# Attention with normalised queries and keys, then an MLP: a planned schedule gets another DMA model, new tables, and denser filler matmuls

## Chip, cores and metric

The kernel runs on one core of a Trainium2 chip. The metric is the device time of one execution in microseconds (us). A core has five engines that run side by side and wait for each other through semaphores: PE (TensorE, matrix products), DVE (VectorE), ACT (ScalarE), POOL (GpSimd) and SP (SyncE, which here only issues transfers). PEld is the loading of weights into PE, which overlaps its products.

## The reference

```python
def _attn_ref(q, k, v, g_q, g_k):            # 8 x 12 x 448 x 64
    q_n, k_n = rmsnorm(q, g_q), rmsnorm(k, g_k)
    scores = np.matmul(q_n, k_n.transpose(0, 1, 3, 2)) / np.sqrt(64)
    attn = softmax(scores)
    return np.matmul(attn, v)

def reference(...):
    x = attn_out.transpose(0, 2, 1, 3).reshape(3584, 768)
    h = x @ w_in                              # 768 x 2048
    g = h * np.clip(h + 3.0, 0.0, 6.0) / 6.0
    return g @ w_out                          # 2048 x 768
```

`rmsnorm` divides each row of 64 by the root of its mean square (plus 1e-06) and multiplies by the gains. All inputs and the output are float32.

## The kernel before

There are eight batches of twelve heads. Two heads make a pair, so there are 6 pairs in a batch and 48 in all. For a pair, q and k are loaded (`loads`), squared and summed over 64 elements (`prep`, L576 and L593), turned into reciprocal roots on ACT (L599, L600), scaled to bf16 (`qks`, L609 and L616), transposed into `kq` (on PE at L669 for the first two batches, by a DMA at L688 for the rest), and the keys with the gains become `kp`. The values are copied to bf16 with a column of ones (`va`). Scores S are products of `kp` with `kq` (L817), exponentials `e` are taken by ACT (L850), and `e` times `va` gives X with the sums of the softmax in the extra column (L906). DVE normalises X (`xn`, L924 and L925), and `xn` is transposed into `xT` (on PE at L946 for the first two batches, else by a DMA).

A sequence has 448 rows, 3 x 128 + 64. The last 64 keys of each pair, the rest, are handled apart: `kr` and `vr` are loaded for six pairs at once, `kb` holds the scaled rest keys, L822 makes their scores, `er` their exponentials and L788 their part of X.

The MLP of a batch runs on PE between the attention steps of the next one. An h group (L985) is 6 products of 384 or 512 columns into one of two M banks, followed by ACT (`t`, L991) and DVE (`gT`, L993). A y group (L1010) is 16 products of 384 columns, followed by a copy `y` and a store. The weights `w_in_sb` and `w_out_sb` are loaded by eight transfers of 768 KB of bf16 results that POOL issues (L500, L506); they convert from float32. All other transfers are issued by SP, except for two tiny ones for the gains by ACT.

The order is not written by hand. The kernel first records all work as steps (`add`), each with the engines that it may run on and what each costs, a due time and its dependencies. A planner, `Plan`, then simulates list scheduling: it goes forward in time, starts on each engine the ready step with the earliest due time, and repeats this with due times taken backward from the end. At the end three hand-fitted tables act on single steps by their number: `NUDGES` shifts a due time, `ENGINES` fixes the engine, `HOLD` sets the earliest start. The instructions are emitted in the planned order. On the chip each engine works through its list in this order and waits where a semaphore is not there yet. So the planner's times are not obeyed on the chip; only its order is.

The planner's picture of transfers is the class `Queues`. A transfer enters the engines `ENTER` = 1.15 us after its issue on SP, or `SOFT` = 2.0 us after on POOL. Transfers at the heads of different rings share the engines. When a POOL transfer comes up after a time without one, it has the engines for itself for `ALONE` packets per engine (18 the first time, 3 later).

Where the planned order leaves PE open for more than 0.2 us before 115 us, `fill` puts in zero matmuls (L1128): products of zeros into a part of a PSUM bank that nobody reads then, with 240 columns (in X) or 64 (in S). They keep PE busy. They have no data to wait for but stand in PE's list like all others, so they take their time whether the gap is there or not. `FILL` = 0.9 scales how many there are for a gap, `FILL_FROM` = 1.2 is where filling starts, and up to `COLD` = 7.0 us each counts double. Ahead of everything DVE sets `zero` (L1136) and three whole PSUM tiles, X, S0 and S1 (L1138), to zero.

Of the kernel before, what the change touches and what calls it, by code (L numbers as in the profile page):

```python
# [19 lines left out]


NUDGES = {
    9: -1709, 10: -818, 11: -16, 12: -13, 13: -178, 14: -247, 15: -51, 16: -1.32, 17: -134, 18: -210,
    20: -10.58, 21: -79, 22: -61, 33: -65.1, 34: -65, 36: 99, 38: 94, 41: 151, 42: 323, 47: -56, 52: 1, 53: -50,
    54: -11, 58: -56, 60: -444, 64: -31, 71: -15, 72: -12, 82: -3.5, 85: -1677, 98: 91, 110: 30, 138: 396,
    140: 946, 172: -194, 179: 112, 193: 197, 196: 33, 197: -208, 205: -525, 227: 20, 230: -1329, 241: -553,
    242: -347, 251: -1753, 277: -127, 283: 31, 288: 134, 289: 242, 291: 544, 295: 406, 301: -130, 338: 28,
    342: -80, 347: -703, 357: -294, 368: 9, 369: 377.5, 370: 375, 376: 243, 377: 229, 381: -2085, 383: -240,
    409: 72, 423: 734, 431: -357, 441: -5, 447: 108, 450: -678, 451: 112, 457: -140, 458: -110, 484: -5,
    489: -22, 491: -74, 498: -325, 499: -319, 501: -8, 521: -15, 522: -8, 528: 322, 536: 10, 537: 34, 552: -12,  # L30
    565: 19, 583: 2.3, 594: 27, 617: -9, 655: -22, 671: -643, 672: -92, 673: -81, 685: 4, 693: 22, 703: 32,
    705: -129, 706: -560, 718: 23, 720: 138, 740: 21, 769: -490, 770: -26, 771: -7, 773: 19, 783: -25,
    784: -760, 792: 22, 801: 57, 802: 25, 804: -54, 805: -11, 811: 13, 840: 43, 861: 23, 870: -194, 871: -56,
    885: -3, 906: -171, 916: 49, 963: -24, 965: -43, 982: 109, 1013: 36, 1029: 45, 1030: -62, 1041: -24,
    1042: -5, 1053: 3.5, 1108: -45, 1132: 15, 1135: -4, 1136: -16, 1146: -91, 1147: -129, 1177: -9, 1179: -4,
    1184: -97, 1204: 4, 1214: 3, 1232: -18, 1233: -8, 1251: -4, 1307: 6, 1337: 2.4, 1379: -16, 1384: -12,
    1387: -2, 1398: -5, 1401: -11, 1408: 11, 1410: 8, 1455: 26, 1468: -21, 1469: -14, 1470: -45, 1471: -10,
    1485: 5.3, 1495: -15, 1520: 6, 1530: -32, 1531: -18, 1562: -21, 1568: -10, 1585: 5, 1604: -15, 1633: -6,
    1649: 5, 1650: 12, 1664: 4, 1669: -47, 1676: 10, 1695: 5, 1697: 3, 1714: -12, 1715: -6, 1716: -4, 1721: -3,
    1722: -4, 1742: -6, 1756: -5, 1774: -1, 1844: -4, 1848: 11, 1855: -13, 1875: -6, 1876: -8, 1893: -6,  # L40
    1919: 8, 1924: -4, 1940: -2, 1984: -9, 1997: 10, 2003: 2, 2016: -11, 2026: -2, 2027: -2,
}
ENGINES = {
    55: "POOL", 56: "ACT", 57: "POOL", 61: "POOL", 69: "DVE", 70: "DVE", 75: "ACT", 76: "DVE", 79: "POOL",
    89: "ACT", 90: "ACT", 91: "DVE", 97: "DVE", 98: "POOL", 102: "POOL", 115: "DVE", 120: "POOL", 123: "DVE",
    124: "POOL", 128: "POOL", 138: "ACT", 152: "POOL", 156: "POOL", 176: "ACT", 177: "POOL", 180: "POOL",
    184: "ACT", 185: "DVE", 189: "ACT", 211: "ACT", 223: "DVE", 240: "DVE", 244: "ACT", 252: "DVE", 253: "DVE",
    272: "DVE", 273: "POOL", 293: "DVE", 314: "ACT", 335: "ACT", 345: "DVE", 346: "DVE", 366: "ACT", 369: "DVE",
    370: "DVE", 376: "ACT", 404: "ACT", 430: "DVE", 495: "ACT", 525: "ACT", 583: "POOL", 689: "POOL",
    774: "DVE", 833: "DVE", 948: "DVE", 1123: "DVE", 1188: "POOL", 1209: "DVE", 1218: "POOL", 1386: "POOL",  # L50
    1750: "POOL",
}
HOLD = {
    39: 42.73, 40: 33, 41: 32, 47: 1, 58: 1, 62: 19, 109: 38, 110: 44, 150: 27, 177: 33, 207: 37, 227: 62,
    270: 36, 271: 36, 282: 42, 320: 46.7, 326: 85.2, 327: 53, 337: 24, 360: 56, 366: 51.1, 394: 62, 409: 44,
    410: 64, 411: 68, 412: 87, 413: 81, 448: 14, 465: 62, 476: 69, 526: 16, 527: 21, 532: 32, 533: 87, 549: 83,
    550: 82, 555: 53, 556: 86.7, 604: 70, 610: 77, 611: 94, 624: 76, 635: 95, 636: 99, 653: 93.6, 658: 104,
    659: 105, 660: 132, 661: 136, 664: 100, 695: 84, 696: 101, 713: 37, 714: 99, 715: 109.7, 790: 110, 791: 85,
    796: 119, 797: 129.9, 798: 125.233, 817: 111, 818: 97, 827: 112, 872: 97, 882: 140, 883: 89, 884: 125,
    885: 130, 907: 134, 908: 121, 928: 141, 929: 148, 930: 118, 931: 118, 932: 137, 976: 125, 977: 148, 982: 54,  # L60
    984: 154.57, 985: 19, 1006: 146, 1007: 96, 1064: 173, 1069: 179, 1070: 164, 1071: 177, 1100: 180, 1141: 185,
    1155: 163, 1157: 158, 1175: 193, 1193: 141, 1194: 199, 1195: 164, 1196: 206, 1236: 200.38, 1246: 177,
    1248: 178, 1249: 204.4, 1266: 212, 1267: 216, 1286: 183, 1289: 236, 1322: 208, 1329: 229, 1349: 225,
    1370: 232, 1416: 235, 1439: 218, 1440: 213, 1453: 254, 1460: 240, 1461: 195, 1462: 237, 1463: 225,
    1464: 215, 1508: 230, 1516: 243, 1558: 245, 1561: 198, 1596: 266.3, 1601: 280, 1602: 273, 1603: 277,
    1604: 266.5, 1622: 272.97, 1673: 275, 1707: 273, 1726: 303, 1727: 316, 1768: 306, 1781: 303, 1799: 329.7,
    1854: 296, 1860: 288, 1861: 310, 1936: 333, 1937: 333,
}


class Step:
# [5 lines left out]
    def __init__(self, on, due, fn, deps, xfer, after, lock, late, n):  # L77
        self.on, self.due, self.fn, self.xfer, self.after, self.lock = on, due, fn, xfer, after, lock
        self.deps = list({id(d): d for d in deps if d is not None}.values())
        self.late, self.n = late, n  # L80
        self.eng = self.start = self.end = None


class Queues:

    ENTER, SOFT, DONE, FIRST, ROOM = 1.15, 2.0, 0.3, 2.9, 108
    EXTRA, BEHIND = 0.05, 0.6
    ALONE = 18, 3  # L90

    def __init__(self):
        self.now = self.FIRST
        self.rings = {"SP": [], "ACT": [], "POOL": []}
        self.issued = []
        self.alone, self.awake, self.wakes = 0.0, False, 0

    def issue(self, s, at):
        n, size = s.xfer[0:2]
        cost = size * 4.5e-5 if s.eng == "POOL" else 0.012 + size * 4.2e-5  # L100
        n += self.EXTRA / cost
        if len(s.xfer) > 2 and self.rings[s.eng]:
            n += self.BEHIND / cost
        self.rings[s.eng].append([s, n, cost, at + (self.SOFT if s.eng == "POOL" else self.ENTER)])
        if s.eng != "POOL":
            self.issued.append(s)

    def lane(self):


        if sum(s.xfer[-1] if len(s.xfer) > 2 else s.xfer[0] for s in self.issued if s.end is None) > self.ROOM:
            return None
        return self.issued[-8].end if len(self.issued) >= 8 else 0.0

    def advance(self, until):

        while True:
# [5 lines left out]
            if soft and not self.awake:  # L123
                self.alone = self.ALONE[min(self.wakes, 1)]
                self.wakes += 1
# [195 lines left out]
def kernel(  # L321
# [35 lines left out]
    def tiles(name, n, shape, dt=BF16, pool=const):  # L357
# [38 lines left out]
    S_r = Ring(tiles("S", 2, [128, 2, 512], FP32, psum))  # L396
    X_r = Ring(tiles("X", 1, [128, 2, 512], FP32, psum))
    M_r = Ring(tiles("M", 2, [128, 512], FP32, psum))
    idle = [(X_r, 0, X_r.bufs[0][:, 1, 272:512]), (S_r, 0, S_r.bufs[0][:, 0, S:512]),
            (S_r, 1, S_r.bufs[1][:, 0, S:512])]  # L400
# [1 line left out]
    plan = Plan(NUDGES, ENGINES, HOLD)  # L402
    add = plan.add

    FILL, FILL_FROM, FILL_TO, COLD = 0.9, 1.2, 115.0, 7.0
    XPE, TQ, MOVE = 2, 0.26, 12
    GATE, W_IN_AT, W_OUT_AT, W_STEP = 4, 6.0, 40.0, 4.3
    START, FIRST, PAIR = 9.0, 3.7, 2.1
# [725 lines left out]

    with tc.manual_schedule():
        nc.vector.memset(zero[:], 0.0)  # L1136
        for t in (X_r.bufs[0][:], S_r.bufs[0][:], S_r.bufs[1][:]):
            nc.vector.memset(t, 0.0)  # L1138
        holder, free = None, FILL_FROM
        for s in order:  # L1140
            if s.eng == "PE":
                if s.start < FILL_TO and s.start - free > 0.2:
                    fill(free, s.start - 0.1, s.start)
                free = s.end
            ins = s.fn(s.eng)
            if ins is not None and s.lock and s.eng in ("DVE", "POOL"):
                if s.eng == "POOL" and holder is not None:
                    tc.add_manual_dep(ins.ins, holder.ins.name, mybir.DependencyInfo(
                        mybir.DependencyClass.Sync, mybir.DependencyReason.DATA), reason="port")
                holder = ins if s.eng == "DVE" else None  # L1150
# [30 lines left out]
```

## Time and profile before

| | us |
|---|---|
| median of 9 executions | 436.12 (434.15 to 438.27) |
| the profiled execution | 434.81 |
| its span, first to last instruction | 432.9 |
| PE busy | 419.4 |
| first zero matmul on PE starts | 2.16 |
| first scores on PE start | 11.89 |
| first h group's products start | 44.1 |
| first y group's products start | 78.3 |
| last of the weight transfers issued | 53.5 |

The page of a profile gives the busy time of each engine and groups of instructions. Busy is the union of the instructions' durations, and a matmul's duration includes its way through the array (a zero matmul of 240 columns lasts 0.266 us, but 22 of them in a row take 2.43). A row in the timeline has start, length, engine, line, operation and count; in square brackets stands how long the engine was idle before it and what ended that. The start of the timeline reads:

```profile
0.83 0.16 DVE L1136 MEMSET zero<- 128x120 uint32 x1 [0.83 <-PEq L1165]
1.20 0.91 DVE L1138 MEMSET X<- 128x1024 f32 x1 [0.21 <-issue]
2.16 3.56 PE L1128 MATMUL X<-zero 128*128 128x240 bf16 x17 [2.16 <-DVE X L1138]
2.27 0.91 DVE L1138 MEMSET S<- 128x1024 f32 x1 [0.16 <-issue]
3.35 0.91 DVE L1138 MEMSET S<- 128x1024 f32 x1 [0.16 <-issue]
3.40 0.58 ACT L574 ACTIVATE sq<-kf 128x448 f32<-128x448 f32 x1 [1.38 <-DMA kf<-in_k_dram]
5.09 0.28 DVE L483 SCALAR_TENSOR_TENSOR grow<-grow 1x128 f32<-1x128 f32 x1 [0.78 <-DMA grow<-in_g_k_dram]
```

### The profile page before, as it was taken

To read this page: it belongs to the slowest core of one execution; us is meant where nothing else is said; L and a number is where in the kernel's file an instruction comes from. 1 tells how busy PE (TensorE), PEld (TensorE's weight loads), DVE (VectorE), ACT (ScalarE), POOL (GpSimd) and SP (SyncE) were. 2 spreads that over 40 slices of the span, in tenths; PEclk is the share of its full clock that TensorE was granted. 3 is DMA by queue.
4 is the path that set the end of the run, shared out by engine and by line. 5 is a ranking of instruction groups with operands and counts; after the bars stand their busy time and mean duration, and the time that the engine had idled before them with its cause. 6 is when DMAs were issued, how large, how long until landed. Compare 5 with 4: busy or idle time off the path is not lost.

```text
span 432.9 us, 10404 instructions
## 1 busy us (share of the span) xinstructions
PE 419.4 (97%) x4174; PEld 248.7 (57%) x4191; DVE 239.3 (55%) x465; ACT 249.7 (58%) x458; POOL 217.5 (50%) x273
## 2 busy tenths in 40 slices
PE   7988999999999999999999999999999999999995
PEld 5666666565456565655556566554556665644563
DVE  7786887346765574556664665356645454244300
ACT  5887877467883687427763767337765565023211
POOL 4657556786869453676755754744847400000000
PEclk9999999999999999999999999999999999999999
DMA  8999999869876959695697784776562712310122
GB/s 237 212 228 258 247 230 212 166 170 223 191 162 159 204 120 186 114 245 117 117 198 200 136 162 134 150 197 177 95 156 74 120 26 50 82 47 0 38 73 74
DMA packets 114840, 64.79 MB, mean 150 GB/s; under 512 B 71272, under 2 KB 111336, under 8 KB 114792
## 3 DMA queue, kind: packets, MB, share of 16 engines
q1 hardware_dynamic: 107488, 57.83, 59.2%
q0 software_dynamic: 7296, 6.29, 9.1%
q8 instruction: 33, 0.54, 0.5%
q14 instruction: 15, 0.12, 0.1%
q10 hardware_dynamic: 8, 0.00, 0.0%
HBM read 45.61 MB, written 11.01 MB: 131 GB/s over the span
## 4 chain that ended last, share of the span: by engine, by line
PE 85%; DMA 6%; DVE 4%; ACT 2%; issue 1%; POOL 1%; SPq 1%; POOLq 0%; DVEq 0%; ACTq 0%
PE M L985 28%; PE M L1010 28%; PE X L906 8%; PE S L817 7%; PE S L1010 4%; PE S L985 2%; DMA kr<-in_k_dram 2%; DMA qf<-in_q_dram 2%; PE S L822 2%; PE X L1010 2%; DMA vf<-in_v_dram 2%; PE X L985 1%; PE X L788 1%; DVE ssq L593 1%; ACT e L850 1%
## 5 line engine op out<-in xcount | busy, mean ns | idle before, releaser
L985 PE MATMUL M<-xT,w_in_sb 128*128 128x384 bf16 (+1 forms) x681 | 143.5, 349 | 1.5 <-DVE gT L993 0.7
L850 ACT ACTIVATE e<-S 128x896 bf16<-128x896 f32 x144 | 124.9, 914 | 21.7 <-PE S L817 21.4
L1010 PE MATMUL M<-w_out_sb,gT 128*128 128x384 bf16 x736 | 130.0, 326 | 0.0
L1010 PEld LDWEIGHTS <-gT 128*128 128x128 bf16 x896 | 84.9, 98 | 55.2 <-issue 0.7
L985 PEld LDWEIGHTS <-w_in_sb 128*128 128x128 bf16 x768 | 70.9, 98 | 62.9 <-issue 3.2
L993 DVE SCALAR_TENSOR_TENSOR gT<-t,M 128x384 bf16<-128x384 f32 (+1 forms) x116 | 71.0, 613 | 62.6 <-ACT t L991 61.5
L991 ACT ACTIVATE t<-M 128x384 f32<-128x384 f32 (+1 forms) x116 | 62.7, 540 | 64.8 <-PE M L985 63.9
L593 DVE TENSOR_REDUCE ssq<-sq 128x14 f32<-128x896 f32 (+1 forms) x49 | 51.6, 1061 | 5.9 <-POOL sq L576 4.9
L906 PEld LDWEIGHTS <-e 128*128 128x128 bf16 x1152 | 45.3, 98 | 14.0 <-issue 5.5
L576 POOL TENSOR_TENSOR sq<-qf 112x512 f32<-112x512 f32 (+1 forms) x43 | 43.8, 1023 | 15.9 <-DMA qf<-in_q_dram 9.7
L906 PE MATMUL X<-va,e 128*128 128x65 bf16 x1152 | 51.7, 194 | 0.1
L540 DVE COPY y<-M 128x384 f32<-128x384 f32 x38 | 21.2, 558 | 43.4 <-PE M L1010 43.4
L817 PE MATMUL S<-kq,kp 64*128 64x448 bf16 x288 | 41.2, 354 | 1.7 <-ACT e L850 1.1
L576 POOL TENSOR_TENSOR sq<-kf 128x384 f32<-128x384 f32 (+1 forms) x39 | 32.4, 835 | 18.7 <-DMA kf<-in_k_dram 6.8
L616 POOL TENSOR_TENSOR qks<-kf,rs 128x384 bf16<-128x384 f32 x36 | 29.9, 831 | 21.6 <-ACT rs L600 17.0
L625 POOL TENSOR_TENSOR qks<-qf,rs 112x512 bf16<-112x512 f32 x36 | 37.6, 1046 | 4.2 <-ACT rs L600 3.7
L540 POOL CAST va<-vf 128x384 bf16<-128x384 f32 x44 | 22.2, 508 | 30.9 <-PE X L906 13.9
L850 ACT ACTIVATE er<-S 128x896 bf16<-128x896 f32 (+1 forms) x27 | 22.5, 833 | 18.9 <-PE S L822 18.8
L691 POOL TENSOR_SCALAR kp<-kq,gp 128x384 bf16<-128x384 bf16 x16 | 20.7, 1295 | 14.2 <-PE S L817 10.2
L925 DVE TENSOR_TENSOR xn<-X,rd 128x384 bf16<-128x384 f32 x48 | 26.8, 558 | 1.9 <-DVE rd L924 0.2
L599 ACT ACTIVATE rs<-ssq 128x14 f32<-128x14 f32 (+1 forms) x49 | 10.5, 214 | 24.0 <-DVE ssq L593 23.7
L817 PEld LDWEIGHTS <-kp 64*128 64x128 bf16 x288 | 9.4, 94 | 21.2 <-issue 18.0
(80 smaller groups left out, 313.0 us busy)
## 6 DMA issues: line engine op xcount, KB each, us to landing
qf<-in_q_dram SPq DMA_DIRECT2D x48, 224.0 KB, 3.7
kf<-in_k_dram SPq DMA_DIRECT2D x36, 192.0 KB, 3.5
vf<-in_v_dram SPq DMA_DIRECT2D x36, 192.0 KB, 3.6
out_dram<-y SPq DMA_DIRECT2D x18, 192.0 KB, 3.1
w_in_sb<-in_moe_w_in_dram POOLq DMA_DIRECT2D x4, 768.0 KB, 12.9
w_out_sb<-in_moe_w_out_dram POOLq DMA_DIRECT2D x4, 768.0 KB, 19.0
kf<-in_k_dram SPq DMA_DIRECT2D x12, 224.0 KB, 5.2
vf<-in_v_dram SPq DMA_DIRECT2D x24, 96.0 KB, 8.9
```

Source lines behind the costliest of these rows:

```text
L540: return (nc.vector if e == "DVE" else nc.gpsimd).tensor_copy(out=out, in_=x)
L576: return engines[e].tensor_tensor(out=o, in0=x, in1=x, op=MULT)
L593: lambda i0=i0, i1=i1, rows=rows: nc.vector.tensor_reduce(out=ssq[0:rows, i0:i1], in_=sq[0:rows, i0:i1], axis=AX_X, op=ADD),
L616: return engines[e].tensor_tensor(out=qks[:, 0:NS].rearrange("p t (h d) -> p h t d", h=2), in0=kf[:, 0:KH].rearrange("p (h t) d -> p h t d ...
L625: return engines[e].tensor_tensor(out=qks[0:PT, NS:QB].rearrange("p t (h d) -> p h t d", h=2), in0=qf[0:PT].rearrange("p (h t) d -> p h t ...
L817: fns.append(lambda ps=ps, a=a, t=t, kp=kp, rhs=rhs: nc.tensor.matmul(out=ps[:, a, 0:S], lhsT=kp[a * 64:a * 64 + 64, t * 128:(t + 1) * 128 ...
L850: lambda dst=dst, ps=ps, w=2 if whole else 1: nc.scalar.activation(out=dst, in_=ps[:, 0:w, 0:S], func=EXP), s, *(AVW[P] if t < NS else AVR ...
L906: nc.tensor.matmul(out=X[:, a, s * E1:(s + 1) * E1], lhsT=e[:, t, a, c0:c0 + 128], rhs=va[:, a * NS + t, :], start=False, stop=(t == NS - ...
L985: nc.tensor.matmul(out=m[:, 0:n], lhsT=w_in_sb[:, kt, f * 128:(f + 1) * 128], rhs=X[:, kt, :], start=(kt == 0), stop=(kt == NKT - 1))
L991: r = add("ACT", 0.17 + n / 1200, due + span, lambda: nc.scalar.activation(out=t[:, 0:n], in_=m[:, 0:n], func=RELU, bias=0.5, scale=1.0 / ...
L993: g = add("DVE", 0.155 + n / 960, due + span, lambda: nc.vector.scalar_tensor_tensor(out=G[:, f, :], in0=t[:, 0:n], scalar=1.0, in1=m[:, 0 ...
L1010: nc.tensor.matmul(out=m[:, 0:HALF], lhsT=G[:, f, i * 128:(i + 1) * 128], rhs=w_out_sb[:, f, cols], start=(f == 0), stop=(f == NFT - 1))
```

## The change

Four things change. In the planner's model the first POOL transfer enters after 1.75 us and each later one after 3.7 us (`SOFT` was 2.0 for all), and `ALONE` is 21 and 4 packets instead of 18 and 3. The three tables are made anew under this model, so the order on all engines, and the engine of some steps, differs; no step is added or removed. `FILL` is 1.0 and `FILL_FROM` 0.8. And before the start only those parts of X, S0 and S1 are set to zero that the zero matmuls write: 240, 64 and 64 columns instead of three times 1,024. The three tables are cut here; nearly every entry of them changes.

```diff
@@ NUDGES, ENGINES, HOLD
-    9: -1709, 10: -818, 11: -16, 12: -13, 13: -178, 14: -247, 15: -51, 16: -1.32, 17: -134, 18: -210,
+    9: -4221, 10: -2412, 11: -102, 12: -96, 13: -179.2, 14: -317, 17: -179.6, 18: -272, 20: -107, 21: -106,
...
@@ class Queues
-    ENTER, SOFT, DONE, FIRST, ROOM = 1.15, 2.0, 0.3, 2.9, 108
+    ENTER, SOFT, DONE, FIRST, ROOM = 1.15, (1.75, 3.7), 0.3, 2.9, 108
     EXTRA, BEHIND = 0.05, 0.6
-    ALONE = 18, 3
+    ALONE = 21, 4
...
-        self.alone, self.awake, self.wakes = 0.0, False, 0
+        self.alone, self.awake, self.wakes, self.soft = 0.0, False, 0, 0
...
-        self.rings[s.eng].append([s, n, cost, at + (self.SOFT if s.eng == "POOL" else self.ENTER)])
-        if s.eng != "POOL":
+        enter = self.ENTER
+        if s.eng == "POOL":
+            enter = self.SOFT[min(self.soft, 1)]
+            self.soft += 1
+        else:
             self.issued.append(s)
+        self.rings[s.eng].append([s, n, cost, at + enter])
@@ the kernel
-    FILL, FILL_FROM, FILL_TO, COLD = 0.9, 1.2, 115.0, 7.0
+    FILL, FILL_FROM, FILL_TO, COLD = 1.0, 0.8, 115.0, 7.0
...
         nc.vector.memset(zero[:], 0.0)
-        for t in (X_r.bufs[0][:], S_r.bufs[0][:], S_r.bufs[1][:]):
+        for _, _, t in idle:
             nc.vector.memset(t, 0.0)
```

In the built kernels the zero matmuls stand as follows: before 108 of 240 columns and 174 of 64, after 134 and 86. The other 3,909 matmuls are the same ones in another order.

## The prediction

> **What bounds the kernel now.** I read the page's first two parts, then the stretches, then the chain and the waits of TensorE (PE).
>
> ```profile
> PE 419.4 (97%) x4174; PEld 248.7 (57%) x4191; DVE 239.3 (55%) x465; ACT 249.7 (58%) x458; POOL 217.5 (50%) x273
> ...
> PEclk9999999999999999999999999999999999999999
> DMA  8999999869876959695697784776562712310122
> ```
>
> PE is busy 97% of the span at full clock, no other engine above 58%. The next view cuts that by stretch (columns: stretch, length, busy us and instructions of PE, PEld, DVE, ACT, POOL, then clock, DMA share, GB/s):
>
> ```profile
> 0.00:11.89 11.89, 9.47 (x83) 7.16 (x84) 8.78 (x17) 6.14 (x15) 5.46 (x23) 1.00 0.86 235
> 11.89:78.00 66.11, 60.80 (x1058) 42.35 (x1058) 51.67 (x110) 53.49 (x108) 42.28 (x52) 1.00 1.19 229
> 78.00:120.00 42.00, 41.68 (x399) 23.27 (x401) 21.56 (x40) 28.68 (x53) 31.94 (x39) 1.00 0.84 186
> 120.00:400.00 280.00, 279.16 (x2477) 159.79 (x2487) 153.31 (x295) 154.68 (x271) 137.77 (x161) 1.00 0.60 132
> ```
>
> The same stretches, zero matmuls alone:
>
> ```profile
> 0.00:11.89 11.89, 8.74 (x54) 6.28 (x54) 1.00 0.86 235
> 11.89:78.00 66.11, 14.97 (x229) 10.93 (x228) 1.00 1.19 229
> 78.00:120.00 42.00, 0.04 (x1) 0.00 (x0) 1.00 0.84 186
> ```
>
> From 78 us on PE has no filler and, to 400, 1.2 us of idle: nothing is left to win there. Before 78 us it waits: until the first scores (11.89) nearly everything is filler; from there to 78 us 15.0 us are zeros and 5.3 us idle. In that stretch the DMA share is over 1. The chain says what it waits for:
>
> ```profile
> 17.52 7.55 DMA vf<-in_v_dram
> ...
> 64.22 9.09 DMA kr<-in_k_dram
> 73.45 0.83 POOL sqr L738
> ...
> 77.19 0.74 PE S L1128 x20
> ```
>
> and the list of waits shows how little of the 5.3 us is a named wait:
>
> ```profile
> PE X L1128 <- DVE X L1138: 2.2, 1, 2.2
> PE S L817 <- ACT e L850: 1.1, 3, 0.5
> PE M L985 <- DVE gT L993: 0.7, 2, 0.5
> ```
>
> So the end is: start of PE, plus fixed real work, plus what the order leaves open before 78 us. Each microsecond closed there moves the end.
>
> **What the Trainium skill says.** "TensorE: Matmul & The Clock Gate", section Back-to-back issue gap, gives N/2.4 + 2.5 ns warm and N/1.2 cold. The trace agrees: 22 zero matmuls of 240 columns took 2.43 us, less 0.27 for the last one's length, so 0.103 us each; 20 of 64 columns took 0.74, so 0.029; the first 17, cold, about 0.2. Part 1 of that page says that the clock rises after some 3.4 us of activity in a free-running window; here PE starts at 2.16, the twelve zeros from 5.84 still take 0.19 each and those from 8.45 0.103. "VectorE: DVE Perf Modes", section on zero memsets, says one cycle per element; the trace has 0.91 us for 1,024. "DMA: Bandwidth & Descriptors", section Queues, rings and completion order, says that the engines alternate between queues by packets. The trace differs where a weight transfer begins: from 18.8 to 20.6 us the software queue took 107.4% of the engines, the hardware queue 6.3%. This stretch is what ALONE and the entry delay SOFT describe.
>
> **The change part by part.** The instruction order of the built kernels gives counts, the trace durations.
>
> Memsets: X shrinks from 1,024 to 240 columns, S0 and S1 to 64 each. By the 0.91 us row, an estimate of 0.25 for X. It begins at 1.20, so PE starts at about 1.5 and not 2.16, and DVE is free at about 2.0, not 4.26. That alone brings nothing: what follows waits for the first loads (ACT's square at 3.40) and for the gains (DVE at 5.09).
>
> First scores: 54 zeros before (17, 12, 3, 22), 58 after (21, 11, 13, 13). PE: 1.5 + 21 x 0.2 = 5.7, the gain row, 11 zeros of which some 7 cold to 7.9; the first transposes, whose input POOL scales from 6.4 for 0.94, are ready by then; 13 x 0.103 to 9.6, second transposes, 13 x 0.103 to 11.3. DVE: two sums to 6.5, gp, a square to 7.3, kb after the transposes to 8.75, two sums of 1.08 to 10.9, the copy of kp (0.42) to 11.35. First scores near 11.5: -0.4 us, bounds -0.8 and +0.3 (kp is now last on a full DVE).
>
> Zeros after the first scores: before 54 of 240 columns and 174 of 64, 54 x 0.103 + 174 x 0.029 = 10.6 us; after 76 and 86, 10.3 us. Their sum hardly moves; their meaning does. FILL was 0.9, so 10.6 us of zeros stood for gaps of 24,096 columns / 2400 / 0.9 = 11.2 us; at 1.0, 23,744 columns stand for 9.9 us. So the open time of the order falls by 1.3 us. Each gap also keeps 0.1 us plus a remainder (I take 0.15): 26 gaps against 24, -0.3 us. As a check, 11.2 - 10.6 + 26 x 0.15 = 4.5 us, near the 5.3 us of idle: the run followed its order with only about 1 us lost beyond.
>
> Where: up to 116,000 real columns, which PE reached at 78 us, the zeros fall from 10.6 to 8.8 us, above all where the chain waited for kr: from 99,000 to 116,000 real columns 5,712 zero columns become 3,104. Both halves of kr are issued two to three places earlier on SP, and one of the two vf half-loads behind the 17.52 row too. But 15 zeros of 240 columns (9 and 6) come where before had none, in what were 100 to 115 us: 1.55 us given back, since zeros issue whether or not the data came.
>
> Filling gaps whole: 64-column zeros cost 0.029 against the planned 0.0267, 86 x 0.0023 = 0.2 us too long, hidden by the 0.1 us margin of each gap; without it, +0.2.
>
> Entry delay and ALONE: no instruction of their own. Later weights are believed to enter at 3.7 us instead of 2.0, so data is planned later around them. Worth nothing if the old belief was right, and up to the 1 us of unplanned idle above if wrong. I take -0.2.
>
> Work moved between engines (both keys and queries of the first pair now POOL; kp, kb, xT copies traded between ACT and DVE): counts differ by one to three of 0.4 to 0.9 us per kind, on engines at 58% or less. Nothing after 12 us; their cover is PE's zeros, and they come out in the gap count.
>
> After 115 us there are no zeros to count. I compared what lies on PE between a bank's last use and its next: MLP banks have as few short returns after (8 under 1.3 us) as before (7). S banks: 3 and 3. The same 3,909 real matmuls stand there, the last 16-matmul groups unchanged. I take 0; bounds -0.4 (the 1.2 us of idle can't all go) and +2.5 (some five more late returns of 0.5 us, the size of the longest wait shown).
>
> Sum: -0.4 - 1.3 - 0.3 - 0.2 = -2.2 us. The profiled execution took 434.81, 432.9 of it span; its forecast is a span of 430.7 and 432.6 in all. The median of the runs shown is 436.12, 1.3 above it, so the median goes to 433.9. That is -0.5%, just at what a measurement of this kernel can tell from no change (about 0.5%, 2.2 us).
>
> **Rivals.** (a) Slower: a load comes later than its planned place. The order on PE is fixed, so one late load stops everything behind it. Flights in the saturated stretch are already 7.55 and 9.09 us on the chain against medians of 3.5 to 3.7; after issues the first w_in ahead of a value copy and the second and third back to back on POOL. If two loads find those bursts of about 2 us in their way, each 2 us beyond its filled gap, and another microsecond is lost in the late part, it is -2.2 + 5 = +2.8: 438.9. It decides from 2.2 us of such lateness. For it: idle no longer absorbs lateness, as gaps are full. Against: the new order expects the weights later, and kr and vf go out sooner.
> (b) Larger gain: the single stalls (22 to 35 us: a dozen of 0.3 to 0.8 us) and the unplanned microsecond shrink as well, 2 us more: 431.9. For it: the stalls sit where loads and exponentials arrive irregularly. Against: several wait for ACT's e, no matter of DMA.
> (c) No change to speak of: the 1.55 us of new zeros are pure loss and the first scores stay at 11.9 because of kp: -2.2 + 0.4 + 1.3 = -0.5: 435.6.
>
> **How the numbers follow.** Forecast 0.45, (a) 0.22, (b) 0.22, (c) 0.11. The forecast lies on the bound, so half of it (0.22) counts as faster: with (b) 0.44. Slower is (a) and a little of (c)'s spread, 0.23. The rest, 0.33, is no change. Predicted 433.9. The forecast's own range is 432.4 to 435.4. Signs are mixed, so the range takes in (b) down to 430.8 (the stalls' 2 us plus the better bounds of first scores and late part) and (a) up to 438.6, leaving a tenth on each side.
>
> **What would show it.** PE's first zero near 1.5 us; first scores near 11.5; zeros between first scores and the mark of 78 us near 8.8 us of pace and idle near 4; the step after kr about 2 us earlier; 15 zeros between 98 and 115 us; stretches after 120 us as dense as now. Wrong if a new DMA row over 8 us stands on the chain before 78 us, if first scores come after 12, or if idle after 120 us exceeds 2 us.

## The result, and the profile after

| | before | after |
|---|---|---|
| median, first comparison (us) | 434.89 (53 executions) | 436.92 (16) |
| ratio to before, 95% interval | | 1.0037 [1.0021, 1.0053] |
| the same kernel in a later comparison (e9) | 434.95 (30) | 438.05 (6), 1.0070 [1.0050, 1.0091] |
| the profiled execution, its span | 434.81, 432.9 | 437.64, 435.9 |
| first zero matmul on PE starts | 2.16 | 1.35 |
| first scores on PE start | 11.89 | 11.15 |

So the kernel became slower by about 0.4 to 0.7%, not faster by 0.5%. (A ratio here is not the quotient of the two medians: that would be 1.0047 and 1.0071.) In the page of the kernel after PE is busy 420.4 us, 1.0 more than before, of a span that is 2.9 us longer. One slice of its clock, the third (21.8 to 32.7 us), is below 9:

```profile
PE 420.4 (96%) x4113; PEld 248.1 (57%) x4129; DVE 239.8 (55%) x463; ACT 250.2 (57%) x456; POOL 222.9 (51%) x277
...
PEclk9989999999999999999999999999999999999999
```

The stretches of the kernel after have the same columns as those of the kernel before:

```profile
0.00:11.89 11.89, 10.11 (x107) 7.48 (x109) 6.92 (x18) 5.74 (x15) 6.21 (x23) 1.00 0.86 233
11.89:78.00 66.11, 58.69 (x960) 39.01 (x954) 48.57 (x102) 52.46 (x104) 43.85 (x53) 0.97 1.14 219
78.00:120.00 42.00, 40.98 (x382) 23.78 (x383) 24.31 (x48) 27.51 (x53) 28.53 (x36) 1.00 0.86 190
120.00:400.00 280.00, 279.37 (x2503) 160.35 (x2514) 154.46 (x290) 156.34 (x271) 144.27 (x167) 1.00 0.57 134
```

and its zero matmuls alone (stretch, length, busy us and count of PE, then of PEld; later columns are the clock and the transfers of the whole kernel):

```profile
11.89:78.00 66.11, 12.62 (x143) 7.95 (x144) 0.00 (x0) 0.97 1.14 219
78.00:120.00 42.00, 2.46 (x20) 1.68 (x19) 0.00 (x0) 1.00 0.86 190
```

After 120 us PE is as dense as before. Between 11.89 and 78 us it has 2.35 us less of zeros, but idle has grown from 5.3 to 7.4 us, and the mean clock of these 66 us is 0.97 instead of 1.00. To find the place, I counted the columns of real matmuls that PE had done. (The traces of before and after lack 17 and 16 of the 3,909 real matmuls, none of them ahead of 100 us. Counted from the end of the span they do no harm there either.) PE reaches 14,000 columns at 20.10 us (20.19 before) and 25,000 at 30.02 (27.82). Further marks, in us, with three other runs that are explained below (e9 is the kernel after once more; e2 and e7 have the first weight transfer later):

| real columns done | before | after | e9 | e2 | e7 |
|---|---|---|---|---|---|
| 32,500 | 31.11 | 33.81 | 32.97 | 30.48 | 30.56 |
| 50,000 | 43.69 | 45.64 | 46.44 | 41.63 | 41.77 |
| 100,000 | 67.06 | 69.45 | 70.56 | 65.22 | 65.21 |
| 117,000 | 78.06 | 78.80 | 79.78 | 74.56 | 74.45 |
| 160,000 | 95.84 | 97.44 | 97.53 | 94.04 | 93.54 |
| from there to the end | 337.1 | 338.4 | 338.4 | 338.4 | 338.0 |

In this profile the kernel after falls 2.7 us behind between 20 and 33 us. It regains 2 us where the kernel before waited after `kr`, between 100,000 and 117,000 columns. It loses about 0.9 us again up to 160,000 columns and 1.3 us behind them, where the 15 new zeros stand. e9 shows that the place is not fixed: there PE is 1.9 us behind at 32,500 columns and 3.5 at 100,000. Windows of 2 us around the first stall, two lines of before and then after:

```profile
22.00:24.00 2.00, 1.54 (x33) 1.25 (x32) 1.90 (x5) 1.97 (x7) 1.84 (x3) 1.00 1.15 233
24.00:26.00 2.00, 1.97 (x52) 1.58 (x52) 1.85 (x5) 1.30 (x5) 0.07 (x1) 1.00 1.21 252
```

```profile
22.00:24.00 2.00, 0.69 (x6) 0.34 (x6) 1.57 (x3) 1.56 (x3) 0.88 (x2) 1.00 1.10 319
24.00:26.00 2.00, 0.80 (x8) 0.25 (x6) 1.38 (x3) 0.29 (x2) 0.54 (x2) 1.00 1.08 281
26.00:28.00 2.00, 1.98 (x34) 1.67 (x33) 1.10 (x3) 1.75 (x3) 2.00 (x3) 0.52 0.91 177
28.00:30.00 2.00, 1.97 (x32) 1.20 (x32) 1.27 (x4) 1.39 (x3) 1.99 (x3) 0.63 0.98 179
```

PE works 1.49 of 4 us (3.51 before), and then 3.4 us at half the clock: 24 products of L908 took 1.50 us, not 0.94. The chain of the kernel after (start, length, what) tells what PE waited for:

```profile
13.20 0.89 SPq L527
...
15.42 7.58 DMA vf<-in_v_dram
...
31.30 9.55 DMA kf<-in_k_dram
...
56.75 12.08 DMA qf<-in_q_dram
```

And the timeline around the first stall: a row of POOL in before, then, of after, SP and POOL, DVE, PE (idle before the row and its end in brackets):

```profile
15.96 1.05 POOL L500 DMA_DIRECT2D w_in_sb<-in_moe_w_in_dram  x1
```

```profile
12.57 1.52 SPq L527 DMA_DIRECT2D kf<-in_k_dram  x1
...
14.84 0.54 SPq L527 DMA_DIRECT2D qf<-in_q_dram  x1
15.42 0.60 SPq L534 DMA_DIRECT2D vf<-in_v_dram  x1
...
14.19 1.05 POOL L502 DMA_DIRECT2D w_in_sb<-in_moe_w_in_dram  x1
15.46 0.50 POOL L542 CAST va<-vf 128x384 bf16<-128x384 f32 x1 [0.22 <-DMA vf<-in_v_dram]
20.85 0.93 POOL L578 TENSOR_TENSOR sq<-qf 128x448 f32<-128x448 f32 x1 [4.89 <-DVE kp L543]
23.12 0.51 POOL L542 CAST va<-vf 128x384 bf16<-128x384 f32 x1 [1.34 <-DMA vf<-in_v_dram]
23.59 0.94 POOL L578 TENSOR_TENSOR sq<-qf 128x448 f32<-128x448 f32 x1
...
24.55 1.09 DVE L595 TENSOR_REDUCE ssq<-sq 128x14 f32<-128x896 f32 x1 [0.95 <-POOL sq L578]
25.67 0.29 DVE L931 TENSOR_TENSOR xr<-X,rd 64x128 bf16<-64x128 f32 x1
...
26.02 0.40 PE L790 MATMUL X<-var,er 64*128 64x65 bf16 x8 [1.22 <-DVE xr L931]
```

The first weight transfer now leaves POOL at 14.19 us, before it left at 15.96. SP's list is late: in this profile the issue of a key tile at 12.57 took 1.52 us, and the loads of qf and of a half vf left behind the weights. The vf half flew 7.58 us. POOL works in order, so its copy of vf at 23.12 held the square at 23.59. DVE summed that square at 24.55 and, also in order, came to `xr` only at 25.67. PE waited for it until 26.02. (The 4.89 us of idle ahead of 20.85 are put down to `kp`, which DVE finished at 20.84. It was the load: by the list of transfers qf, issued at 14.84, landed 5.9 us later, at 20.74, and in e2 below, whose DVE list is the same, this square ran at 18.72, well before `kp`.)

### The profile page after: what moved, and what is told of

It reads as the page before. It is cut to its first block, busy times and chain, and to the rows that moved or that the text cites. A ratio compares the mean times of both kernels' runs of the same rounds, so it can differ in the third digit from the quotient of the medians.

```text
span 435.9 us, 10293 instructions
## 1 busy us (share of the span) xinstructions
PE 420.4 (96%) x4113; PEld 248.1 (57%) x4129; DVE 239.8 (55%) x463; ACT 250.2 (57%) x456; POOL 222.9 (51%) x277
## 4 chain that ended last, share of the span: by engine, by line
PE 80%; DMA 9%; POOL 5%; DVE 3%; issue 1%; SPq 1%; ACT 1%; POOLq 0%; DVEq 0%; ACTq 0%
PE M L1012 27%; PE M L987 26%; PE X L908 7%; PE S L819 6%; DMA qf<-in_q_dram 4%; PE S L1012 4%; PE S L987 2%; DMA kf<-in_k_dram 2%; POOL qks L611 2%; PE X L1012 2%; DMA vf<-in_v_dram 2%; PE S L824 2%; DVE ssq L595 1%; PE X L987 1%; PE X L790 1%
## 5 line engine op out<-in xcount | busy, mean ns | idle before, releaser
L908 PEld LDWEIGHTS <-e 128*128 128x128 bf16 x1152 | 45.8, 99 | 12.9 <-issue 3.7
L908 PE MATMUL X<-va,e 128*128 128x65 bf16 x1152 | 52.1, 195 | 0.0
L578 POOL TENSOR_TENSOR sq<-qf 112x512 f32<-112x512 f32 (+1 forms) x40 | 41.6, 1041 | 11.7 <-DVE kp L543 4.9
L693 POOL TENSOR_SCALAR kp<-kq,gp 128x384 bf16<-128x384 bf16 x19 | 23.6, 1245 | 26.3 <-PE S L819 15.6
L1130 PE MATMUL X<-zero 128*128 128x240 bf16 x134 | 20.0, 288 | 1.6 <-DVE X L1140 1.3
```

The lines of the kernel that those rows point to most:

```text
L578: return engines[e].tensor_tensor(out=o, in0=x, in1=x, op=MULT)
L908: nc.tensor.matmul(out=X[:, a, s * E1:(s + 1) * E1], lhsT=e[:, t, a, c0:c0 + 128], rhs=va[:, a * NS + t, :], start=False, stop=(t == NS - ...
```

## The experiments

I took up five theories. A: loads issued around the first weight transfer come late, and the engines, each in order, hand the delay to PE. B: zeros that fill whole gaps leave no slack. C: the new order is worse in many places. D: the half clock after PE has waited is a cost of its own. Z: zeros in the gaps cost time in either order. Every ratio is to the kernel before, run on the same chip, with its 95% interval. A profile is one execution, and executions of one kernel differ: those of the kernel after run from 434.69 to 437.74 us.

| kernel | median us | ratio |
|---|---|---|
| e1_loads_first | 435.79 | 1.0017 [0.9994, 1.0040] |
| e2_burst_later | 435.12 | 0.9984 [0.9969, 0.9999] |
| e3_tables_alone | 435.94 | 1.0011 [0.9991, 1.0032] |
| e4_fill_memset | 434.05 | 0.9979 [0.9962, 0.9996] |
| e5_value_behind | 436.72 | 1.0054 [1.0032, 1.0075] |
| e6_zeros_there | 437.56 | 1.0060 [1.0043, 1.0077] |
| e7_later_fill95 | 434.73 | 0.9998 [0.9979, 1.0017] |
| e8_before_early | 435.15 | 1.0006 [0.9993, 1.0019] |
| e9_after_again | 438.05 | 1.0070 [1.0050, 1.0091] |
| e10_burst_mid | 436.08 | 1.0044 [1.0022, 1.0065] |
| e11_fill_undone | 436.57 | 1.0038 [1.0025, 1.0051] |
| e12_no_zeros | 433.10 | 0.9963 [0.9946, 0.9980] |

Medians in this table come from three chips; e1 to e4 shared one, e5 to e8 one, e9 to e12 one. So compare ratios, not medians, across these groups.

**When the first weights go.** All of these move one step of the finished order in the order of emission; `move(n, to)` puts step n ahead of step `to`, with `True` behind it.

```diff
     order = plan.order()
+    move(36, 124, True)     # e2: first weight transfer behind POOL's square of qf
+    move(36, 44, True)      # e10: the same, behind the va copy that followed it
+    move(38, 61)            # e8, in before: first weight transfer ahead of POOL's scaling of q
```

> The changed kernel with the first weight transfer issued on POOL after the square that follows the v copy, so about 5 us later; SP's list as changed. Theory A: the q and v loads issued at 14.8 and 15.4 us no longer meet the weights and land after 3 to 5 us instead of 5.9 and 7.6, POOL goes on by 19.5 us, PE's clock stays at 1 between 20 and 30 us; the weights come 4 to 5 us later, which their first use near 47 us can bear; ratio 0.996 to 1.002. If the late loads come from SP's own delay alone and the weights have no part, they land as late as before and the ratio stays at 1.002 to 1.006. Theory B: 1.002 to 1.006.

> The kernel after, with the first weight transfer put behind the va copy that follows it on POOL, so near 16.0 us instead of 14.2 (the time at which the kernel before issues it; e2_burst_later has it at 19.6). Theory A (the loads issued within some 3 us of that transfer are held): qf at 14.84 and the vf half at 15.42 get ahead of it, half or more of the loss goes: 435.2 to 436.0. Rival (not the time of the transfer, but that fewer weights compete at all in this stretch): 436.5 to 437.

> The kernel before, with its first weight transfer put ahead of the scaling at 13.50 us on POOL, so that POOL issues it some 2 us earlier; nothing else moves. Theory A (loads that SP issues in the 3 us after the first weight transfer are held, and with them POOL, DVE and PE): a stall of 1.5 to 3 us appears between 20 and 35 us also in this order, 436.4 to 438. Rival (it is the new order of the other work, not the time of the transfer): 434.5 to 435.3, as the kernel before.

e2 sends the weights at 19.59 us and the loss is gone: POOL copies vf at 20.64 us (23.12 in after), and `xr` starts at 23.48 (25.67). PE reaches 32,500 columns at 30.48 us (31.11 before the change, 33.81 after it) and 117,000 at 74.56 (78.06, 78.80). Its windows over the same place:

```profile
22.00:24.00 2.00, 1.64 (x19) 0.76 (x18) 1.94 (x4) 1.97 (x6) 2.00 (x4) 1.00 0.95 136
24.00:26.00 2.00, 2.00 (x45) 1.34 (x39) 1.68 (x5) 2.00 (x4) 1.51 (x3) 1.00 1.16 192
26.00:28.00 2.00, 1.77 (x57) 1.54 (x56) 1.44 (x5) 1.52 (x4) 2.00 (x4) 1.00 1.13 265
```

PE is busy 5.41 of 6 us, at full clock. This is what theory A asks for; the rest of the new order, its filler and its memsets are untouched. In this profile SP also happened to be 2 us earlier (qf at 12.80, the vf half at 13.38). e7 below, with the same late weights, has them at 14.35 and 14.93, only 0.5 us earlier than after, and no stall either, so SP's delay alone does not make it.

That the lead at 117,000 columns, 3.5 us, shrinks to 0.5 us of span has two reasons. The 15 zeros take their time later. And at 80 us comes another wait of the same kind: a load of qf that SP issued at 70.42 flew 7.17 us, POOL squared it at 77.77, DVE summed it at 78.85 and came behind it to `xT`:

```profile
80.83 0.30 PE L790 MATMUL X<-var,er 64*128 64x65 bf16 x8 [1.44 <-DVE xT L542]
```

The same wait is 1.16 us in e7 and 0.71 in after; before and e9 have none there.

e10 sends the weights at 16.29 and also passes the first place (32,500 columns at 30.48), but its profile has a second one:

```profile
40.00:42.00 2.00, 0.13 (x4) 0.00 (x1) 0.76 (x2) 0.38 (x1) 1.99 (x3) 1.00 1.17 207
42.00:44.00 2.00, 1.70 (x34) 1.60 (x35) 0.56 (x2) 0.62 (x2) 1.57 (x3) 0.65 1.16 213
44.00:46.00 2.00, 2.00 (x11) 1.06 (x10) 1.87 (x4) 1.41 (x2) 0.55 (x2) 0.50 1.22 213
```

with POOL as follows:

```profile
38.63 0.93 POOL L578 TENSOR_TENSOR sq<-kf 128x448 f32<-128x448 f32 x1 [1.78 <-DMA kf<-in_k_dram]
39.51 0.89 POOL L502 DMA_DIRECT2D w_in_sb<-in_moe_w_in_dram  x1
40.39 0.89 POOL L508 DMA_DIRECT2D w_out_sb<-in_moe_w_out_dram  x1
41.29 0.96 POOL L611 TENSOR_TENSOR qks<-qf,rs 128x448 bf16<-128x448 f32 x1
```

The pattern is that of 23 us: POOL idle 1.78 us for a load, then two weight issues of 0.89 us in a row, then the scaling for which PE waits 2.2 us until 42.30, then 3.4 us at half clock. This place is not e10's own. The kernel after waits 0.8 us there in its first profile, and in e9, where the first stall is milder (PE works 2.60 of 4 us from 22 to 26, at full clock), this is where its half clock lies:

```profile
42.00:44.00 2.00, 0.71 (x23) 0.58 (x19) 1.14 (x3) 0.96 (x2) 1.99 (x4) 1.00 1.14 232
44.00:46.00 2.00, 1.20 (x28) 1.14 (x29) 0.00 (x0) 0.59 (x2) 1.93 (x3) 0.71 1.12 198
```

```profile
44.80 0.56 PE L671 MATMUL M<-ident,qks 64*64 64x64 bf16 x14 [2.08 <-POOL qks L611]
```

In e2 POOL has the same list there, but kf is in time (it squares it at 36.05 without waiting for the load), and PE waits for nothing longer than 0.3 us. The time of e10, 436.08, is just above what theory A expected, and its interval overlaps that of e9, so that it saves a part of the loss is likely, not certain.

e8 is a miss for the simple form of theory A: the same early transfer in the old order (13.80 us) costs nothing that can be measured. So an early weight transfer does harm only together with the new order. That the loads which PE needs next stand behind it there is argued, not tested. In e8 SP had issued kf at 12.98 and vf at 13.93, and the 16 DMA engines stayed full; in the kernel after SP was behind, and they ran nearly dry from 14.0 to 14.7 us. The dry stretch is not needed for the loss: in e9 it lasts 0.15 us at this place.

**Which load.** Two kernels change single steps in the order after.

```diff
+    move(54, 53); move(19, 53)   # e1: loads of qf and a half vf ahead of the key reload on SP
+    move(55, 98, True)           # e5: POOL's late va copy behind the next square
```

> The changed kernel, with two loads (the q load that the square of 20.85 us waits for, and the second half of the v load that the copy of 23.12 us waits for) issued on SP two to four places earlier, ahead of the k load that took 1.5 us to issue; all else in the changed order. Theory A (these two loads come 2 us late out of SP's list, fall behind the first weight transfer, and hold POOL, then DVE, then PE): the v copy on POOL runs before 20 us instead of 23.12, no stretch of 2 us between 20 and 30 us shows a PE clock under 1, PE passes its 32,500th real column at least 1.5 us earlier than the changed kernel's 33.8 us, and the time falls by 1.5 to 3 us from the changed kernel's, to 433.5 to 435.5 or a ratio of 0.996 to 1.001. Theory B (zeros that fill gaps whole hold PE back all along): no change, ratio 1.002 to 1.006. Theory C (the new order is worse in many places): under 1 us gained, ratio 1.001 to 1.004.

> The kernel after, with one POOL copy (the va copy that stood at 23.12 and waited for a load until then) put behind the square that followed it. Theory A (late load, then in-order engines): the square no longer waits for that load, so its sum on DVE, xr and the first product after the stall at 26.02 come 1 to 1.7 us earlier, and TensorE may keep its clock; PE reaches 32,500 real columns near 31.5 instead of 33.8, the time is 434.6 to 435.6. Rival (the load itself is what the products need, whatever stands behind it): the stall only changes its name, PE at 32,500 columns stays within 0.5 us of 33.8 and the time at 436.9.

Neither did all that was expected. In e1 the next half vf, issued at 14.91, became the late one (6.42 us), its copy held ACT, and PE waited 1.8 us for `er`. That profile is of one of the longer executions (437.83 us). Seven of e1's 14 executions have a mean clock of 0.997 or more and take 435.04 us on average, the other seven 437.39: so e1 helps in a part of its executions. In e5 POOL got past its old stop, and PE reached 32,500 columns at 32.22 us, 1.6 us earlier than in after. But POOL stood at the next load:

```profile
24.00 0.93 POOL L578 TENSOR_TENSOR sq<-kf 128x448 f32<-128x448 f32 x1 [3.29 <-DMA kf<-in_k_dram]
24.88 1.72 POOL L502 DMA_DIRECT2D w_in_sb<-in_moe_w_in_dram  x2
27.03 0.93 POOL L611 TENSOR_TENSOR qks<-kf,rs 128x448 bf16<-128x448 f32 x1 [0.43 <-DMA vr<-in_v_dram]
```

PE waited 1.9 us for `xn` until 27.53, and its longest wait came at the second place, behind two weight issues at 42.23 and 43.12:

```profile
45.02 0.58 PE L671 MATMUL M<-ident,qks 64*64 64x64 bf16 x14 [3.06 <-POOL qks L611]
```

(The profile is of the slowest of six executions, 439.00 us.) So it is not one load or one copy that is late: several loads behind the weights are, and whoever needs the next one stops. Theory C is right in a small part: the order after stops at 20 to 33, at 40 to 46 and at 80 us and spends time on zeros at 100 and 112 us, but from 120 us on it is as dense as before.

**The parts of the change, alone.**

```diff
-    FILL, FILL_FROM, FILL_TO, COLD = 1.0, 0.8, 115.0, 7.0
+    FILL, FILL_FROM, FILL_TO, COLD = 0.9, 1.2, 115.0, 7.0    # e3, e11: in after
-        for _, _, t in idle:
+        for t in (X_r.bufs[0][:], S_r.bufs[0][:], S_r.bufs[1][:]):    # e3 only
```

e4 is the opposite: the kernel before with these two edits the other way round. e7 is the kernel of e2 with `FILL_TO` 95 instead of 115.

> The changed model and tables with the filler constants (0.9 from 1.2 us) and the three whole memsets of before. Theory A: the late loads are in the tables, so the loss stays: ratio 1.002 to 1.008, and PE's gap between 21 and 26 us is there. Theory B (the denser zeros are the loss): ratio 0.993 to 0.999.

> The kernel before with the other two parts alone: filler 1.0 from 0.8 us, and small memsets; its own model and tables. Theory A: harmless, ratio 0.997 to 1.001; the first zero on PE at about 1.5 us. Theory B: the whole loss is here, ratio 1.002 to 1.006.

> The kernel after, with FILL 0.9 and FILL_FROM 1.2 again; the small memsets and the new order stay. Theory B (in this order, whose loads come late, gaps filled whole leave PE nothing to catch up with): 0.5 to 1 us faster than the kernel after, 436.0. Theories A and D: the stall stands as it is, within 0.4 us of the kernel after.

> The kernel of e2_burst_later, with filling ended at 95 us instead of 115 us: the 15 zero matmuls at 98 to 113 us are gone, nothing else differs. Theory (they are pure loss, 15 x 0.103 us): 433.6, 1.5 us under e2_burst_later, and PE as dense after it. Rival (they stand in a gap that is there anyway): 435.1, the time of e2_burst_later.

In the old order denser filler and small memsets are a small gain (e4), so theory B fails as a general rule. In the new order undoing the filler gave 1.5 us against e9 on the same chip, with intervals that just touch; e3, with neither, can't be told from before, though its profile, an execution of 437.58 us, has the first stall (32,500 columns at 35.35). So the filler seems to add to the loss where loads come late, and this is not settled.

For e7 the profiles say more than the medians, which come from two chips and show no gain over e2. The nine zeros at 100 us cost their time in full: from 160,000 to 170,000 columns PE takes 4.99 us with them (e9) and 4.07 without (e7, and e12 in the old order). The six at 112 us do not: without them PE takes 4.65 us from 190,000 to 200,000 columns, with them 4.73, and e7 waits another 0.5 us soon after. From 160,000 columns to the end e7 is 0.46 us faster than e2. The six profiles of the old order take 336.9 to 337.1 us for this part, the eleven of the new order with zeros there 338.3 to 338.6. So some 1.4 us of the new order's loss lie here, in every profile, and have nothing to do with late weights.

**Repeating after, zeros and the clock.**

```diff
+                for _ in range({153: 5, 148: 8, 167: 11}.get(s.n, 0)):    # e6, in after
+                    nc.tensor.matmul(out=spare_m[:, 0:240], lhsT=zero[:, 0:128], rhs=zero[:, 0:240],
+                                     start=True, stop=True, skip_group_check=True)
-                if s.start < FILL_TO and s.start - free > 0.2:
+                if s.start < FILL_TO and s.start - free > 0.2 and not 12 < s.start < 40:    # e12, in before
```

> The kernel after, unchanged, on the chip of the three runs sent with it, to compare them with. Theories A and D both expect its stall between 20 and 33 us again and a time near 436.9, with a mean clock under 0.997 in most of its executions; if it is an accident of the chip that ran it first, 434.5 to 435.5.

> The kernel after, with 24 more zero matmuls of 240 columns (5, 8 and 11) at the three places between 21.7 and 26.0 us where PE waited for 0.62, 0.94 and 1.22 us; they write a part of PSUM that nobody uses then. 24 x 0.103 = 2.5 us of zeros against 2.8 us of waiting. Theory D (part of the loss is that the clock halves after PE has waited): PE stays busy, the clock stays at 1.00, PE reaches 32,500 real columns 1.3 to 1.8 us earlier, the time is 435.3. Rival (the loss is the waiting alone): nothing moves or it gets slower by up to 0.3 us, 436.9 to 437.2.

> The kernel before, without the zero matmuls planned between 12 and 40 us (30 of 240 columns and 42 of 64, 4.3 us at their pace); all else stays. Theory D (PE that has waited gets half the clock for some us): windows with a clock near 0.5 appear between 15 and 40 us, the mean clock of most executions falls under 0.997 and the time rises by 1 to 2.5 us, 436 to 437.3. Rival (zeros only take time, what PE waits for sets the pace): no lower clock, 434.0 to 435.0.

e9 repeats the loss on another chip, though with its stalls shared out otherwise, as shown above. e6 kept PE busy from 22 to 26 us, as meant, and the clock stayed at 1.00 there. But in its profile kf came still later (POOL idle 3.05 us until 26.97), the wait moved to 28 to 31 us and the half clock, 6.8 us of it, behind it. Nothing was gained. Four of its ten executions kept a mean clock of 0.997 or more and still took 437.05 us on average: the waits alone are enough for the loss. e12 is the surprise: it is the fastest in this table, although its clock does what theory D said:

```profile
16.00:18.00 2.00, 0.64 (x6) 0.16 (x3) 1.74 (x4) 1.95 (x5) 0.85 (x2) 0.93 1.10 236
18.00:20.00 2.00, 1.72 (x27) 0.85 (x28) 0.00 (x0) 2.00 (x4) 2.00 (x3) 0.50 1.17 205
20.00:22.00 2.00, 2.00 (x32) 1.08 (x28) 1.59 (x4) 1.17 (x4) 2.00 (x4) 0.50 1.18 202
22.00:24.00 2.00, 2.00 (x23) 1.11 (x20) 1.93 (x4) 1.87 (x5) 1.28 (x2) 0.50 1.13 252
```

Half the clock for 6.8 us costs nothing that can be seen here: ACT is busy 1.95 and 2.00 us of the windows in which PE has 0.64 and 1.72, and the tenth exponential `e` ends at 27.00 us against 27.23 before. Both readings that I had put up were half right: the clock falls, and the time falls too. A low mean clock (under 0.997 in 14 of 17 executions of after, and all six of e9; in 45 of 179 of before) is thus a sign that PE has waited, not by itself the loss. In the kernel before the executions with a low clock take 1.4 to 2.1 us more than the others on each of the four chips. So the old order may have such a stall too, only less often; no such execution of it was profiled (the profile of before has 0.998, that of after 0.996), and so this is not shown.

**Do zeros or loads make the loss?** Four last kernels set the two against each other within one comparison.

```diff
-    nc.sync.dma_start_transpose(out=kq[:], in_=qks[:].rearrange("p t c -> p (t c)"))
+    nc.sync.dma_start(out=kq[:], in_=qks[:])         # h1 to h4, and so at the other three places
+                if s.start < FILL_TO and s.start - free > 0.2 and not 12 < s.start < 40:    # h2, h4
```

> The kernel before, with its 86 transposing transfers (the first at 67 us) made plain copies of the same size, so that queries, keys and X of the later batches stay untransposed and the output of these is another; everything up to 67 us is as before. A base for the other three of this call. The plain copies may take less of the queue: 432 to 436, and PE's first 67 us as in the kernel before.

> h1_before_plain without the zero matmuls planned between 12 and 40 us, as e12_no_zeros. Theory Z (zeros that fill gaps delay the end): 1 to 2 us under h1_before_plain, as e12_no_zeros was 1.85 under its base. If that gain came from the transposes' luck after 67 us: within 0.5 us of h1_before_plain.

> The kernel after, with the same 86 transfers made plain copies (untransposed data in the later batches). The loss arises before 67 us by theories A and Z: 2 to 3 us over h1_before_plain. If it arose with the transposes: within 0.5 us of it.

> h3_after_plain without the zero matmuls planned between 12 and 40 us (42 of 240 columns and 38 of 64, 42 x 0.103 + 38 x 0.029 = 5.4 us at full pace). Theory Z (a gap filled whole leaves PE no slack, so a late load is added to the end): 1.5 to 2.5 us under h3_after_plain. Theory A alone (the late loads are the whole loss, zeros only stand beside them): within 0.5 us of it. Theory D (without zeros the clock falls more often and costs time): over it.

| kernel | median us | ratio |
|---|---|---|
| h1_before_plain | 434.07 | 0.9971 [0.9955, 0.9987] |
| h2_before_plain_no_zeros | 433.42 | 0.9944 [0.9922, 0.9966] |
| h3_after_plain | 436.47 | 1.0027 [1.0004, 1.0051] |
| h4_after_plain_no_zeros | 435.50 | 1.0007 [0.9988, 1.0027] |

h3 is 2.4 us above h1 (436.47 less 434.07): the loss of the new order is there without the transposing transfers, which start at 67 us. Taking the zeros from 12 to 40 us out gives 0.65 us in the old order and 0.97 in the new one, both in the direction of theory Z and of e12, each less than its intervals can tell. h4 is still 2.1 us above h2 (435.50 less 433.42). So most of the loss stays without these zeros. It is not all a matter of loads: by the profiles 1.5 us of the distance between h1 and h3, and 1.7 of that between h2 and h4, lie behind 160,000 columns, with the zeros at 100 and 112 us.

## Why the prediction was wrong

The direction was wrong, and rival (a), held at 0.22, was what happened. It gave +2.8 us; the two comparisons give 1.6 us (0.0037 x 434.89) and 3.0 (0.0070 x 434.95). Its mechanism, late loads that stop an order full of zeros, is what the profiles show. That its size fits is partly luck: it set two loads at 2 us each and another microsecond in the late part against the whole gain of 2.2 us, while between e2 and after 4.2 us are lost up to 117,000 columns (78.80 less 74.56; 5.2 to e9).

- First scores: forecast -0.4 us, measured -0.74 in after (11.15 against 11.89). The same head has them at 11.42 in e9, 11.27 in e7 and 11.77 in e2, so the forecast lies within what executions differ by. PE's first zero came at 1.35, near the 1.5 forecast.
- Fewer and better filled gaps: by the forecast's own terms PE should be some 3.7 us earlier at the mark of 78 us (the 2.2 of the sum, and the 1.55 that it gives back later). Where the loads are in time it is: 3.50 us earlier at 117,000 columns in e2, 3.61 in e7. In after it is 0.74 us later. (The forecast put 116,000 columns at 78 us; the trace of before has them at 76.00, ahead of 2 us of waiting and zeros that end at 78.06.) That idle would be "near 4" did not hold: 7.4 us.
- 15 new zeros: they stand where they were counted, and in the profiles 0.92 us of their 1.55 is lost in full; the rest fills a wait (e7).
- After 115 us: taken as 0. PE is busy 279.37 of 280 us from 120 to 400 us, 279.16 before. Right.
- The step that failed is "Entry delay and ALONE", priced at -0.2 us as "worth nothing if the old belief was right, and up to the 1 us of unplanned idle above if wrong". It asked only what the new belief may save. It did not ask what an order made under it does when the loads come later than planned. The first weight transfer left 1.8 us earlier, loads that PE needed soon stood behind it, and where -0.2 was put, the profiles have +4.2 us between e2 and after. The remark that before "followed its order with only about 1 us lost beyond" was carried over to the new order without a reason. Even e2, with the stalls undone, gains only 0.16%: the wait for a late qf at 80 us, 1.4 us, was not in the sum either.
- The argument used against (a), "the new order expects the weights later, and kr and vf go out sooner", took the plan's times for SP's. SP was behind in after and in e9 (both finish the issue of that kf at 14.1 us), and its loads, not the weights, were late. The argument for (a), that full gaps absorb nothing, fits e11, but its size is open.
- "DMA: Bandwidth & Descriptors", cited in the forecast for how queues alternate, did not fit the trace of before at 18.8 us, as the forecast itself noted. From 18 to 20 us of after, the software queue had 93.4% of the engines and the hardware queue 23.7%. That reading was in hand and was used for one sentence, not for a price.
- One of the signs of being wrong came: two new rows over 8 us stand on the chain before 78 us, kf with 9.55 and qf with 12.08. The chain of e2 has such a qf too (11.88), so a long flight on the chain is not by itself the loss. First scores came before 12, and idle after 120 us stayed under 2 us.

What stays open: which property of the new order makes the early transfer harmful, when e8 shows that the old one bears it. SP's delay before 14 us differs between executions of the same head (four halves of vf took SP 3.41 us in after, 2.57 in e2, 3.65 in e7), and no run held it fixed. Of all versions that compute the same, the kernel before without its zeros from 12 to 40 us (e12) was the fastest, at 0.9963 of the time before; it was not combined with later weights in the new order.

## What to carry to other kernels

Where a schedule is made by a model of transfers, check on the trace which loads stand within a few microseconds behind a large transfer on another queue, and which in-order engine waits for them: such a wait is passed on by every engine that it touches. Here moving one load or one copy only moved the stall, and moving the transfer in front of them all removed it. Filler matmuls should earn their place in a measurement: here nine of them cost their full time, and half the clock for 6.8 us cost nothing that could be seen where another engine was full. And profile more than one execution before saying where the time is lost: two profiles of the same kernel had their stalls in different places.

## What the runs showed of the hardware

The half clock came in units. In the traces it lasted 3.41 us in after, e9 and e10 and 6.83 us in e1, e5, e6 and e12. "TensorE: Matmul & The Clock Gate", Part 1, speaks of a free-running window of about 3.4 us and of half clock after an idle one. The lengths agree: from the first rise of the clock to its fall after lasts 20.48 us, 6 times 3.413, e9 37.55, 11 times that. But PE need not have been idle. Cut by this grid, the first 100 us of the 18 traces have 13 windows at full clock that are followed by one at half; PE was busy in them for 0.80 to 1.73 of 3.41 us (1.25 in after). No full-clock window there in which PE was busy 1.89 us or more was followed by half clock. So in these traces a window about half busy was the limit.

In most traces SP stopped for about a microsecond at one place in the stretch from 12 to 16 us, not always at the same load. The list of queues of after for 12 to 14 us has one packet of a third queue just there:

```profile
q8 instruction: 1, 0.02, 4.6%
```

In after this transfer of 16 KB ran from 12.24 to 13.71 us, and the issue of kf from 12.57 to 14.09. In e5 it ran from 12.52 to 13.75 (an issue from 12.66 to 14.15), in e6 from 13.80 to 14.96 (13.90 to 15.35). "Runtime: NRT & Kernel Launch", section Instruction fetch mechanics, says that instructions are refilled in blocks of 16 KiB through a queue of their own, mostly hidden. If the coincidence is the cause, it was not hidden here. No run tested that, and three traces speak against a fixed rule: in e4, e8 and e9 such a packet ran (11.76 to 13.07, 15.25 to 16.46, 12.51 to 13.73 us), and no issue of SP beside it took over 0.7 us.
